# A fused attention and MLP kernel: key norms in the exp's scale, the first batch staged ahead of the weights, one copy per transposed tile, and another order around the layer norm

## The chip, the cores and the metric

The kernel runs on one core of a Trainium2 chip. Its time is the device time of one execution in microseconds. TensorE (PE) multiplies matrices and transposes, VectorE (DVE) works on tiles and reads PSUM, ScalarE (ACT) applies functions with a scale and a bias, GpSimd (POOL) works on SBUF and issues the weights' transfers, and SyncE (SP) issues most other transfers.

## The reference

Attention over 8 batches of 12 heads, 448 tokens and 64 dimensions, with q and k divided by their root mean square; then, over the 768 values of each token, a layer norm and an MLP with 3072 hidden values, added to its input.

```
q_n, k_n = rmsnorm(q, g_q), rmsnorm(k, g_k)     # x / sqrt(mean(x*x) + 1e-6) * g
scores = matmul(q_n, k_n.T) / 8;  attn = softmax(scores)
x = matmul(attn, v)                             # [8, 448, 768] after the heads are put side by side
xn = (x - mean) / sqrt(var + 1e-6) * g_ln
out = x + relu(xn @ w_ch1) @ w_ch2
```

## The kernel before

**Attention.** Two heads make a pair; there are 48 pairs, six for each batch. The 448 tokens of a head lie as 384 (three tokens on each of 128 partitions) and 64 left over, and the left-over tokens of two heads share a tile, so a pair has seven tiles of 128 keys. q, k and v come in *units*: one pair each in batch 0 (units 0 to 5), two pairs each later (`UNITS`). `load_unit` issues nine transfers for a unit, one large and two small ones for each of k, q and v. Batch 0's units use three places in the MLP buffer `hT` in turn, so unit 3 waits until unit 0 has been used up; later units have a pool of two (`p_in`).

`prep_ops` makes a unit ready: squares (ACT), sums (DVE), the product of k with both gains (`kg`, POOL), the reciprocal root (`root`: `_rsqrt`, an exp on the bits as a first guess, then six small VectorE steps), `kn` and `qn` (the scaled k and q), `khi` and `klo` (k split into two fp16 halves), `qdup` (q a second time, beside itself) and the copies of v (POOL). `trans_k` and `trans_q` transpose seven tiles on TensorE into one PSUM tile and copy them to SBUF with two and three copies. `scores(p, i)` multiplies one tile of 128 keys by 448 queries and takes the exp on ACT; `values(p, i)` multiplies the result by v, with a column of ones for the sum; after the seventh tile `evac_o` divides. `stats` takes the layer norm's statistics of that pair's 128 columns.

**MLP.** For batch b, `ln_ops` gives the statistics' root, then for each of 3 or 4 token tiles a normalisation (ACT, then DVE) and `ln_trans` (six transposes and a copy to `xnT`). An even batch has 3 token tiles; the left-over 64 tokens wait for the odd batch, which has 4. `mlp_chunks` is 24 *up* chunks (six matmuls, then a relu to `hT`) and 8 *down* chunks for each token tile (six matmuls each).

**Order.** PE, ACT, POOL and SP follow the order in which the program emits; VectorE's order is made by a scheduler. `attention` emits pairs in steps of one key tile: the scores of pair p beside the values of pair p-1, the next units' preparation at planned steps (`todo`). `run` emits attention through pair 6, then the layer norm of batch 0, and then for each batch its MLP chunks with attention steps between them, so that the next batch's attention is done when 0.82 of the chunks' cost (`frac`) is out; the layer norm of the next batch follows, spread over the rest. The weights are issued on POOL, w1 in three transfers and w2 in two, beside pairs 0 and 3.

Transfers from SP and ACT share eight semaphores (DMAHW0 to 7) in turn, so that each issue waits until the transfer eight places before it is complete.

Of the kernel before, what the change touches and what calls it, by code (L numbers as in the profile page):

```python
# [22 lines left out]
UNITS = [(0, 2 * i, 1) for i in range(NPAIR)]  # L23
# [5 lines left out]
REC_LO, REC_HI = 1.0 / 3.0e7, 0.5  # L29


def _rsqrt(nc, out, a, t, eps):

    eng = nc.vector
    eng.tensor_scalar(out=a, in0=a, scalar1=eps, scalar2=None, op0=ALU.add)
    nc.scalar.activation(out, a.bitcast(INT32), AFT.Exp, scale=-0.5 * LN2 * 2.0 ** -23,
                         bias=0.5 * LN2 * (127.0 - 0.043))
    for _ in range(2):
        eng.tensor_tensor(out=t, in0=out, in1=out, op=ALU.mult)  # L39
        eng.scalar_tensor_tensor(out=t, in0=t, scalar=-0.5, in1=a, op0=ALU.mult, op1=ALU.mult)  # L40
        eng.scalar_tensor_tensor(out=out, in0=t, scalar=1.5, in1=out, op0=ALU.add, op1=ALU.mult)
# [14 lines left out]
class _Fast:  # L56


    def __init__(self, ctx, tc, sh, q, k, v, g_ln, w1, w2, out):
# [21 lines left out]
        for t in self.kT:  # L81
            nc.vector.memset(t[:, 1], 0.0)
# [5 lines left out]
        nc.vector.memset(self.rec, 0.01)  # L88
        self.hT = fix.tile([128, NFF, 512], FP16, name="hT", tag="hT")
        self.xs, self.xls, self.st = {}, {}, {}  # L90
# [3 lines left out]
    def load_unit(self, u):  # L94
# [3 lines left out]
        if m == 1:  # L98
            o = 2688 * (u % 3)
            t = self.hT.rearrange("p f n -> p (f n)")[:, o:o + 2688].bitcast(FP32)  # L100
            t = t.rearrange("p (n g d) -> p n g d", n=3, d=D)
        else:
            t = self.p_in.tile([128, 3, 14, D], FP32, tag="qkv")
        eng = nc.scalar if u < 2 else nc.sync
        for n, src in ((1, self.k), (0, self.q), (2, self.v)):
            nc.sync.dma_start(
# [7 lines left out]
    def prep_ops(self, u):  # L114
# [8 lines left out]
        def begin():  # L123
# [3 lines left out]
            c["rt"] = self.p_n.tile([128, 2, 14], FP32, tag="rt", name="rt")[:, :, 0:g]  # L127
            c["qn"] = self.p_n.tile([128, 14, 2, D], FP16, tag="qn", name="qn")[:, 0:g]
# [12 lines left out]
        def root():  # L141
            _rsqrt(nc, c["rr"], c["ssq"], c["rt"], D * 1e-6)
# [6 lines left out]
        def kn():  # L149
            _scaled(nc, c["t"][:, 1], c["t"][:, 1], c["rr"][:, 1])  # L150

        def khi():
            nc.vector.tensor_copy(out=c["khl"][:, :, 0], in_=c["t"][:, 1])
# [5 lines left out]
        def qn():  # L159
            _scaled(nc, c["qn"][:, :, 0], c["t"][:, 0], c["rr"][:, 0])  # L160

        def qdup():
            nc.vector.tensor_copy(out=c["qn"][:, :, 1], in_=c["qn"][:, :, 0])
# [5 lines left out]
        def vleft():  # L169
            for e in range(2):  # L170
# [4 lines left out]
                lambda: (total(0), vmain()), root, None, kn, khi, klo, qn, qdup, vleft]  # L175


    def trans_k(self, p):
# [3 lines left out]
        ps = self.ps_tr.tile([128, 1024], FP16, tag="tr", name="psK")  # L182
        kT = self.kT[p % 2]
        gs = [6 * m + w] + [6 * w + i for i in range(6)]
        for i, g in enumerate(gs):
            nc.tensor.matmul(ps[:, ts(i, 128)], khl[:, g], sh.id16, is_transpose=True,  # L186
                             start=(i == 0), stop=(i == 6))
        flat = kT.rearrange("p g d -> p (g d)")
        nc.vector.tensor_copy(out=flat[:, 0:64], in_=ps[:, 0:64])
        nc.vector.tensor_copy(out=flat[:, 128:960], in_=ps[:, 64:896])  # L190

    def trans_q(self, p):
# [3 lines left out]
        ps = self.ps_tr.tile([128, 1024], FP16, tag="tr", name="psQ")  # L196
        qT = self.p_qT.tile([128, 896], FP16, tag="qT")
        gs = [6 * w, 6 * w + 1, 6 * w + 2, 6 * m + w, 6 * w + 3, 6 * w + 4, 6 * w + 5]
        for i, g in enumerate(gs):
            nc.tensor.matmul(ps[:, ts(i, 128)], qn[:, g], sh.id16,  # L200
                             is_transpose=True, start=(i == 0), stop=(i == 6))
        nc.vector.tensor_copy(out=qT[:, 0:448], in_=ps[:, 0:448])  # L202
        nc.vector.tensor_copy(out=qT[:, 448:832], in_=ps[:, 512:896])
        nc.vector.tensor_copy(out=qT[:, 832:896], in_=ps[:, 448:512])
        self.prs[p] = dict(qT=qT, kT=self.kT[p % 2])

    def scores(self, p, i):
# [11 lines left out]
        else:  # L219
            nc.tensor.matmul(ps[:, 0:S], kT[:, 0:128], qT[:, 0:S], start=True, stop=False)  # L220
            nc.tensor.matmul(ps[:, 0:S], kT[:, 64:192], qT[:, S:2 * S], start=False, stop=True)
        nc.scalar.activation(out=c["E"][:, i], in_=ps[:, 0:S], func=AFT.Exp, scale=1.0 / 8.0,  # L222
                             bias=EXP_BIAS)
# [44 lines left out]
    def attention(self):  # L268

        n, nu = B * NPAIR, len(UNITS)  # L270
        todo, last = {}, -9
        for u in range(1, nu):
            p, m = UNIT_PAIR[u], UNITS[u][2]
            st, e = max(7 * (p - 1 - m) + 2, last + 1), 7 * (p - 1) + 1
            last = e
            ops = self.prep_ops(u)
            for x, op in enumerate(ops):
                if op is not None:
                    todo.setdefault(max(0, st + (e - st) * x // (len(ops) - 1)), []).append(op)
            if u + 2 < nu and u + 2 > 2:  # L280
                todo.setdefault(max(0, e), []).append(lambda u=u: self.load_unit(u + 2))
        for u in range(3):
            self.load_unit(u)
        for op in self.prep_ops(0):
            if op is not None:
                op()
        self.trans_k(0)
        self.trans_q(0)
        for p in range(n + 1):
            b = p // NPAIR  # L290
            if p < n and p % NPAIR == 0:
                self.xs[b] = self.p_x.tile([128, 3, DM], FP32, tag="x", name="x")
                if b % 2 == 0:
                    self.xls[b // 2] = self.p_xl.tile([128, DM], FP32, tag="xl", name="xl")
            for i in range(7):
                for op in todo.pop(7 * p + i, ()):
                    op()
                if p < n:
                    self.scores(p, i)
                if p > 0:  # L300
                    for x in {0: (), 1: (0, 1)}.get(i, (i,)):
                        self.values(p - 1, x)
                if p > 1 and i == 1 and (p - 1) % NPAIR:
                    self.stats(p - 2)
                if p + 1 < n and i == 2:
                    self.trans_k(p + 1)
                if p + 1 < n and i == 4:
                    self.trans_q(p + 1)
                if p > 0 and p % NPAIR == 0 and i == 6:
                    self.stats(p - 1)  # L310
                yield p + (i + 1) / 7
# [7 lines left out]
    def load_w2(self, n0, n1):  # L319
        self.nc.gpsimd.dma_start(  # L320
            out=self.sh.w2[:, n0:n1],
            in_=self.w2[128 * n0:128 * n1].rearrange("(c p) d -> p c d", p=128))
# [8 lines left out]
    def stats(self, p):  # L331
# [3 lines left out]
        if hp == 0:  # L335
            self.st[b] = self.p_m.tile([128, 4, NPAIR * 6 + 2], FP32, tag="stat", name="stat",
                                       bufs=2)
        for t, x in enumerate(self.tok_tiles(b)):
            nc.vector.bn_stats(out=self.st[b][:, t, 6 * hp:6 * hp + 6],  # L339
                               in_=x[:, 128 * hp:128 * hp + 128])  # L340

    def ln_ops(self, b):
# [7 lines left out]
        mv = st[:, :, 6 * NPAIR:6 * NPAIR + 2]  # L350

        def root():
            c["rs"] = self.p_m.tile([128, 4], FP32, tag="rs", name="rs", bufs=2)
            c["sh"] = self.p_m.tile([128, 4], FP32, tag="sh", name="sh", bufs=2)
            for t in range(n):
                nc.vector.bn_aggr(out=mv[:, t], in_=st[:, t, 0:6 * NPAIR])
# [11 lines left out]
        res = [root, lambda: norm(0)]  # L368
        for t in range(1, n):
            res += [lambda t=t: norm(t), lambda t=t: self.ln_trans(c["xn", t - 1], t - 1)]  # L370
        return res + [lambda: self.ln_trans(c["xn", n - 1], n - 1)]
# [11 lines left out]
    def mlp_chunks(self, b):  # L383
# [32 lines left out]
        for t in range(n):  # L416
            for g in range(2):
                for s in range(4):
                    yield 6 * 160, (lambda t=t, g=g, s=s: down(t, g, s))
# [10 lines left out]
    def run(self):  # L430
        att = self.attention()
        self.pos = 0.0

        def upto(target):
            while self.pos < target:
                nxt = next(att, None)
                if nxt is None:
# [240 lines left out]
```

## Time and profile before

| | before |
|---|---|
| median of 3 runs (lowest to highest) | 733.85 us (733.62 to 735.27) |
| the profiled execution, its own time | 733.03 us |
| its span | 731.2 us |
| PE busy | 633.3 us (87%), 5066 matmuls |
| DVE busy | 428.0 us (59%) |
| ACT busy | 338.2 us (46%) |
| POOL busy | 89.7 us (12%) |
| mean granted clock of TensorE | 0.956 |
| DMA packets | 54.83 MB |

A page of the profile gives busy time per engine, the span in 40 slices of 18.3 us (each digit a busy share in tenths), the chain of waits that ended last, and groups of like instructions: line, engine, operation, tiles written and read, count, then busy time, mean of one in ns and the idle time before them with what ended it. In the waits, the name left of the arrow waited for the one right of it: total in us, times, longest. SPq, ACTq and PEq are the queues in which an engine issues transfers or waits.

### The profile page before, as it was taken

The numbers are of one execution on the slowest core, as the hardware profiler recorded it, in microseconds if no ns is written. First come the engines' busy times: TensorE is split into PE (matmuls) and PEld (weight loads), VectorE is DVE, ScalarE is ACT, GpSimd is POOL, SyncE is SP. The second block draws the span as 40 slices with busy tenths as digits, with TensorE's granted clock in tenths as the row PEclk, the third lists the DMA queues.
The fourth block names the chain that finished last, engine by engine and source line by source line (L and its number), as shares of the span: only waits on it lengthen the run. The fifth ranks groups of instructions, "written<-read, shape, count | busy, mean of one in ns | idle before, by whom it ended". The sixth has DMA issues, their size and how long they took to land.

```text
span 731.2 us, 12852 instructions
## 1 busy us (share of the span) xinstructions
PE 633.3 (87%) x5066; PEld 387.3 (53%) x5066; DVE 428.0 (59%) x1195; ACT 338.2 (46%) x646; POOL 89.7 (12%) x119
## 2 busy tenths in 40 slices
PE   0452458997999999997999999998999999979996
PEld 0231335664555666664556666654556566644463
DVE  1886688667466756776646757784565755351011
ACT  1443246753465327752665247633664356423400
POOL 1332012110101101110111011110111010000000
PEclk9997568998999999999999999998999999999999
DMA  4499951221322014230322123202313100000011
GB/s 138 95 220 219 229 150 48 53 77 44 98 77 74 26 44 106 70 99 22 98 76 78 44 85 110 77 23 70 99 28 98 44 22 2 23 23 22 1 44 46
DMA packets 69234, 54.83 MB, mean 75 GB/s; under 512 B 23216, under 2 KB 63152, under 8 KB 69168
## 3 DMA queue, kind: packets, MB, share of 16 engines
q1 hardware_dynamic: 62320, 43.86, 21.0%
q0 software_dynamic: 5456, 9.44, 7.0%
q8 instruction: 41, 0.67, 0.4%
q10 hardware_dynamic: 1392, 0.66, 0.3%
q14 instruction: 25, 0.20, 0.1%
HBM read 52.36 MB, written 11.01 MB: 87 GB/s over the span
## 4 chain that ended last, share of the span: by engine, by line
PE 74%; DVE 11%; DMA 6%; SPq 3%; ACT 3%; issue 1%; ACTq 0%; DVEq 0%
PE psH L394 30%; PE psC L405 25%; PE psS L217 6%; PE oA L241 4%; SPq L111 3%; PE psQ L200 2%; DMA t<-in_k_dram 2%; PE psK L186 2%; DMA hT<-in_q_dram 2%; PE psX L379 2%; PE oB L243 1%; DMA hT<-in_v_dram 1%; ACT t L364 1%; DVE xn L366 1%; DVE x L258 1%
## 5 line engine op out<-in xcount | busy, mean ns | idle before, releaser
L405 PE MATMUL psC<-w,hT 128*128 128x384 f16 x1344 | 246.8, 332 | 0.0
L394 PE MATMUL psH<-xnT,w 128*128 128x512 f16 (+1 forms) x1152 | 245.2, 352 | 1.2 <-DVE xnT L381 1.2
L222 ACT ACTIVATE E<-psS 128x448 f16<-128x448 f32 x336 | 179.1, 540 | 119.9 <-PE psS L217 99.1
L396 ACT ACTIVATE hT<-psH 128x384 f16<-128x384 f32 (+1 forms) x192 | 104.5, 544 | 149.7 <-PE psH L394 148.2
L405 PEld LDWEIGHTS <-hT 128*128 128x128 f16 x1344 | 127.7, 100 | 75.8 <-issue 6.2
L394 PEld LDWEIGHTS <-w 128*128 128x128 f16 x1152 | 105.0, 98 | 81.7 <-issue 1.3
L217 PE MATMUL psS<-qT,kT 128*128 128x448 f16 x288 | 105.3, 373 | 8.0 <-ACT E L222 5.2
L241 PEld LDWEIGHTS <-E 128*128 128x128 f16 x1008 | 74.4, 101 | 68.5 <-issue 20.8
L145 POOL TENSOR_TENSOR t<-t,gprod 128x896 f32<-128x896 f32 x21 | 43.7, 2081 | 455.0 <-issue 271.7
L241 PE MATMUL oA<-v,E 128*128 128x65 f16 x864 | 70.7, 198 | 9.9 <-DVE x L258 9.5
L409 DVE TENSOR_TENSOR x<-psC,x 128x384 f32<-128x384 f32 x48 | 26.7, 556 | 83.3 <-PE psC L405 82.9
L186 PE MATMUL psK<-id,khl 128*128 128x128 f16 x336 | 29.2, 232 | 43.6 <-DVE rt L39 23.6
L243 PE MATMUL oB<-v,E 128*128 128x65 f16 x288 | 53.5, 197 | 0.3
L186 PEld LDWEIGHTS <-khl 128*128 128x128 f16 x336 | 21.5, 104 | 44.9 <-issue 23.8
L139 DVE TENSOR_REDUCE ssq<-khl 128x14 f32<-128x896 f32 (+1 forms) x27 | 26.4, 979 | 26.3 <-ACT khl L136 25.8
L202 DVE COPY qT<-psQ 128x448 f16<-128x448 f16 x48 | 18.7, 389 | 38.6 <-PE psQ L200 38.6
L217 PEld LDWEIGHTS <-kT 128*128 128x128 f16 x288 | 29.2, 103 | 22.5 <-DVE qT L202 2.3
L256 DVE RECIPROCAL rec_all<-oA 128x6 f32<-128x6 f32 x48 | 9.3, 193 | 49.3 <-PE oA L241 49.2
L379 PE MATMUL psX<-id,xn 128*128 128x128 f16 x168 | 15.7, 243 | 22.6 <-DVE xn L366 22.6
L339 DVE BATCH_NORM_STATS2 stat<-x 128x6 f32<-128x128 f32 x144 | 34.5, 282 | 0.7
L243 PEld LDWEIGHTS <-E 128*128 128x128 f16 x336 | 33.3, 99 | 1.4 <-DVE xl L263 0.9
L200 PE MATMUL psQ<-id,qn 128*128 128x128 f16 x336 | 29.2, 232 | 4.9 <-DVE kT L190 4.9
(75 smaller groups left out, 594.8 us busy)
## 6 DMA issues: line engine op xcount, KB each, us to landing
out_dram<-x SPq DMA_DIRECT2D x24, 384.0 KB, 2.3
t<-in_k_dram SPq DMA_DIRECT2D x21, 384.0 KB, 3.6
t<-in_q_dram SPq DMA_DIRECT2D x21, 384.0 KB, 4.1
t<-in_v_dram SPq DMA_DIRECT2D x21, 384.0 KB, 4.4
w<-in_moe_w_ch_dram POOLq DMA_DIRECT2D x3, 1536.0 KB, 21.0
w<-in_moe_w_ch_dram POOLq DMA_DIRECT2D x2, 2304.0 KB, 38.1
out_dram<-xl SPq DMA_DIRECT2D x8, 192.0 KB, 3.0
t<-in_k_dram SPq DMA_DIRECT2D x42, 32.0 KB, 3.4
```

The lines of the kernel that those rows point to most:

```text
L145: nc.gpsimd.tensor_tensor(out=c["t"][:, 1], in0=c["t"][:, 1], in1=sh.gprod.unsqueeze(1).broadcast_to([128, g, D]), op=ALU.mult)
L186: nc.tensor.matmul(ps[:, ts(i, 128)], khl[:, g], sh.id16, is_transpose=True, start=(i == 0), stop=(i == 6))
L200: nc.tensor.matmul(ps[:, ts(i, 128)], qn[:, g], sh.id16, is_transpose=True, start=(i == 0), stop=(i == 6))
L217: nc.tensor.matmul(ps[:, 0:S], kT[:, 192 + 128 * i:320 + 128 * i], qT[:, h * S:(h + 1) * S], start=True, stop=True)
L222: nc.scalar.activation(out=c["E"][:, i], in_=ps[:, 0:S], func=AFT.Exp, scale=1.0 / 8.0, bias=EXP_BIAS)
L241: nc.tensor.matmul(oA[:, t, cs], E[:, i, ts(t, 128)], rhs, start=(i == 0 and t == 0), stop=(i == 6 and t == 2))
L243: nc.tensor.matmul(oB[:, cs], E[:, i, 320:448], rhs, start=(i == 0), stop=(i == 6))
L339: nc.vector.bn_stats(out=self.st[b][:, t, 6 * hp:6 * hp + 6], in_=x[:, 128 * hp:128 * hp + 128])
L379: nc.tensor.matmul(ps[:, dc], xn[:, ts(dc, 128)], sh.id16, is_transpose=True, start=(dc == 0), stop=(dc == NDC - 1))
L394: nc.tensor.matmul(ps[:, 0:N], sh.w1[:, dc, ts(f, 128)], xnT[:, dc, 0:N], start=(dc == 0), stop=(dc == NDC - 1))
L396: nc.scalar.activation(out=hT[:, f, 0:N], in_=ps[:, 0:N], func=AFT.Relu)
L405: nc.tensor.matmul(ps[:, 0:384], hT[:, f, ts(t, 128)], sh.w2[:, f, ts(g, 384)], start=(f == 0), stop=(f == NFF - 1))
```

## The change

It has these parts:

- **Key norms.** k is no longer scaled (`kn` goes). The reciprocal root goes to a tile that is kept (`rr_all`, from `_rsqrt`'s new `last`), and the exp of `scores` takes its column for these 128 keys as scale, where it had the constant 1/8. `khi` moves from DVE to ACT and, with `klo`, no longer needs the root. `qdup` goes to POOL for units 0 to 3.
- **Staging.** Batch 0 has four units (one, one, two and two pairs). Units 0 to 2 get places of their own in `hT`, unit 3 and unit 4 go to `p_in`, and all five are issued at the start. ACT issues only unit 0's q; a first exp (`warm`) brings the table load forward; the layer norm's gain is issued behind unit 3. w1 follows at step 2 and w2 at step 21; w2 is loaded by halves of its columns, and batch 0's down chunks take all token tiles of the first half first.
- **Copies.** One PSUM tile (`tr`) is kept for both transposes. The left-over tile is written in two parts, to where it belongs, and one copy takes the whole: 960 columns for k, 896 for q (on ACT for pairs 0, 2 and 4).
- **Order.** Only the six pairs of batch 0 come before its layer norm. `frac` is 0.77. The layer norm's root and first two normalisations come as soon as attention is done; the transposes come last, one ahead of each of the last chunks. Statistics are taken of 256 columns, after every second pair.
- **Flag.** The check of the sums, by which the general path is chosen at the end, also checks the kept roots against `gmax`, and stands after the third chunk of the last MLP.

The core of the diff:

```diff
-UNITS = [(0, 2 * i, 1) for i in range(NPAIR)]
+UNITS = [(0, 0, 1), (0, 2, 1), (0, 4, 2), (0, 8, 2)]
...
-        if m == 1:
-            o = 2688 * (u % 3)
-            t = self.hT.rearrange("p f n -> p (f n)")[:, o:o + 2688].bitcast(FP32)
+        if u < 3:
+            o = 2688 * u
+            t = self.hT.rearrange("p f n -> p (f n)")[:, o:o + 2688 * m].bitcast(FP32)
...
-        eng = nc.scalar if u < 2 else nc.sync
         for n, src in ((1, self.k), (0, self.q), (2, self.v)):
-            nc.sync.dma_start(
+            eng = nc.scalar if u == 0 and n == 0 else nc.sync
+            eng.dma_start(
...
-        def kn():
-            _scaled(nc, c["t"][:, 1], c["t"][:, 1], c["rr"][:, 1])
-
         def khi():
-            nc.vector.tensor_copy(out=c["khl"][:, :, 0], in_=c["t"][:, 1])
+            nc.scalar.activation(c["khl"][:, :, 0], c["t"][:, 1], AFT.Identity)
...
-                lambda: (total(0), vmain()), root, None, kn, khi, klo, qn, qdup, vleft]
+                lambda: (total(0), vmain()), khi, root, klo, None, qn, qdup, vleft]
...
-        nc.vector.tensor_copy(out=flat[:, 0:64], in_=ps[:, 0:64])
-        nc.vector.tensor_copy(out=flat[:, 128:960], in_=ps[:, 64:896])
+        nc.vector.tensor_copy(out=kT.rearrange("p g d -> p (g d)"), in_=ps[:, 0:960])
...
+        if p in (0, 2, 4):
+            nc.scalar.copy(out=qT, in_=ps.rearrange("p e s -> p (e s)"))
+        else:
+            nc.vector.tensor_copy(out=qT, in_=ps.rearrange("p e s -> p (e s)"))
...
-        nc.scalar.activation(out=c["E"][:, i], in_=ps[:, 0:S], func=AFT.Exp, scale=1.0 / 8.0,
-                             bias=EXP_BIAS)
+        nc.scalar.activation(out=c["E"][:, i], in_=ps[:, 0:S], func=AFT.Exp,
+                             scale=self.rr[:, 1, g:g + 1], bias=EXP_BIAS)
...
+        todo.setdefault(2, []).append(lambda: [self.load_w1(c, c + 1024) for c in range(0, FF, 1024)])
+        todo.setdefault(21, []).append(lambda: [self.load_w2(g) for g in range(2)])
...
+            for u in range(3):
+                self.load_unit(u)
+            for op in self.prep_ops(0):
+                if op is not None:
+                    op()
+            self.trans_k(0)
+            self.trans_q(0)
+            self.load_unit(3)
+            self.nc.sync.dma_start(self.sh.gln, self.g_ln.unsqueeze(0).broadcast_to([128, DM]))
+            self.load_unit(4)
...
-        frac = 0.82
+        frac = 0.77
...
+                if items and len(chunks) - i <= len(items):
+                    items.pop(0)()
                 emit()
                 done += cost
...
+                if self.pos >= goal and items is None:
+                    items = self.ln_ops(b + 1)
+                    items.pop(0)()
```

Where instructions stand, at three places. First, ScalarE from its start: `gg` and `gln` are the gains, `hT` holds the loaded unit, `khl` and `qn` take the squares, `rr` the root's first guess, `E` the exp. Before:

```order
L632 DMA gg_65<-in_g_q_dram 128x64
L633 DMA gg_65<-in_g_k_dram 128x64
L442 DMA gln_70<-in_moe_g_ln_dram 128x768
L111 DMA hT_124<-in_k_dram 64x64 x2
L111 DMA hT_124<-in_q_dram 64x64 x2
L111 DMA hT_124<-in_v_dram 64x64 x2
...
L136 ACT_TABLE_LOAD
L136 ACTIVATE khl_157<-hT_124 128x448
L136 ACTIVATE qn_156<-hT_124 128x448
L36 ACTIVATE rr_154<-ssq_153 128x2x7
```

Of the change:

```order
L668 DMA gg_66<-in_g_q_dram 128x64
L669 DMA gg_66<-in_g_k_dram 128x64
L677 ACT_TABLE_LOAD
L677 ACTIVATE warm_65<-ones_63 128x1
L109 DMA hT_128<-in_q_dram 128x2x192
L114 DMA hT_128<-in_q_dram 64x64 x2
L141 ACTIVATE khl_162<-hT_128 128x448
L141 ACTIVATE qn_161<-hT_128 128x448
L155 ACTIVATE khl_162<-hT_128 128x7x64
L37 ACTIVATE rr_159<-ssq_158 128x2x7
L205 COPY qT_191<-tr_129 128x896
```

Fifteen transfers stood ahead of the first square (the dots leave out six small loads of unit 1); now five do, and the table load stands ahead of three of them.

Second, SyncE at unit 3's loads, with the semaphores that each waits for. Before:

```order
L106 DMA hT_124<-in_k_dram 128x2x192 [waits DMAHW6_49,DVE_49]
L111 DMA hT_124<-in_k_dram 64x64 [waits DMAHW7_49]
L111 DMA hT_124<-in_k_dram 64x64 [waits DMAHW0_49]
L106 DMA hT_124<-in_q_dram 128x2x192 [waits DMAHW1_49,Activation_49]
L111 DMA hT_124<-in_q_dram 64x64 [waits DMAHW2_49]
L111 DMA hT_124<-in_q_dram 64x64 [waits DMAHW3_49]
L106 DMA hT_124<-in_v_dram 128x2x192 [waits DMAHW4_49,Pool_49]
```

Of the change:

```order
L109 DMA t_200<-in_k_dram 128x4x192 [waits DMAHW5_49]
L114 DMA t_200<-in_k_dram 64x2x64 [waits DMAHW6_49]
L114 DMA t_200<-in_k_dram 64x2x64 [waits DMAHW7_49]
L109 DMA t_200<-in_q_dram 128x4x192 [waits DMAHW0_49]
L114 DMA t_200<-in_q_dram 64x2x64 [waits DMAHW1_49]
L114 DMA t_200<-in_q_dram 64x2x64 [waits DMAHW2_49]
L109 DMA t_200<-in_v_dram 128x4x192 [waits DMAHW3_49]
```

The waits for VectorE, ScalarE and GpSimd, which had to be done with unit 0, are gone; those for earlier transfers stay.

Third, TensorE at the end of MLP(0): `oB` are the last values of batch 1's attention, `psC` the MLP's down matmuls, `psX` the layer norm's transposes. Before:

```order
L243 MATMUL oB_1812<-vl_115,E_1628 128x130
L405 LDWEIGHTS hT_124
L405 MATMUL psC_1890<-w2_73,hT_124 128x384
...
L405 MATMUL psC_1961<-w2_73,hT_124 128x384
...
L379 LDWEIGHTS xn_1958
L379 MATMUL psX_1979<-id16_58,xn_1958 128x128
```

Of the change:

```order
L248 MATMUL oB_1665<-vl_120,E_1506 128x130
L447 LDWEIGHTS hT_128
L447 MATMUL psC_1726<-w2_78,hT_128 128x384
...
L447 MATMUL psC_1801<-w2_78,hT_128 128x384
...
L421 LDWEIGHTS xn_1774
L421 MATMUL psX_1829<-id16_58,xn_1774 128x128
...
L447 MATMUL psC_1841<-w2_78,hT_128 128x384
...
L421 MATMUL psX_1848<-id16_58,xn_1778 128x128
```

Between `oB` and the first `psX` there were 18 matmuls on `psC`, and there are 42 now; behind that twelve stood between two token tiles' transposes, and now six.

244 lines of the change are left out of this document (132 added, 112 removed).

## The prediction

> **What bounds the kernel now.** I read the busy slices of the page first, then cut the span into stages.
>
> ```profile
> PE   0452458997999999997999999998999999979996
> ```
>
> TensorE is short of work in the first six slices and full almost everywhere after them. The windows by stage (columns: length, busy time of PE, PEld, DVE, ACT and POOL, granted clock, DMA share, GB/s) say the same in numbers; the cuts are the first exp, the first MLP matmul, and the starts of MLP(1), MLP(2) and MLP(3).
>
> ```profile
> 0.00:28.40 28.40, 2.38 (x16) 1.70 (x17) 12.89 (x42) 3.69 (x7) 4.68 (x14) 1.00 0.38 107
> 28.40:117.55 89.15, 44.63 (x390) 28.89 (x389) 66.75 (x187) 39.93 (x79) 24.30 (x33) 0.77 0.90 186
> 117.55:189.77 72.22, 67.56 (x563) 43.34 (x563) 48.23 (x138) 36.55 (x72) 6.74 (x8) 0.95 0.17 50
> 189.77:273.95 84.18, 83.33 (x657) 48.90 (x655) 51.27 (x139) 42.79 (x79) 10.12 (x12) 1.00 0.23 69
> 273.95:347.77 73.82, 69.38 (x613) 45.27 (x612) 51.94 (x146) 40.90 (x80) 10.11 (x12) 0.98 0.26 73
> ```
>
> Up to 117.55 us PE has only 47.0 us of work, at a mean clock of 0.77 in the second stage; behind that it is busy for 83.33 of 84.18 us. So only two things can be won: the start, and the few waits later. TensorE's waits up to 117.55 (first two rows) and after it (third row) name them.
>
> ```profile
> PE psK L186 <- DVE rt L39: 23.6, 1, 23.6
> PE psK L186 <- DVE khl L156: 20.0, 3, 13.8
> PE psX L379 <- DVE xn L366: 19.7, 7, 4.4
> ```
>
> What stands behind the 20.0 us is shown by the chain of waits from 0 to 120 us (start, length, what):
>
> ```profile
> 14.46 1.28 ACT L136
> ...
> 32.31 9.12 DMA hT<-in_v_dram
> 41.44 11.79 DMA hT<-in_q_dram
> 53.25 4.49 SPq L111
> ...
> 59.86 6.53 SPq L111
> ...
> 73.76 16.33 DMA t<-in_k_dram
> ```
>
> From 32 to 90 us the path is loads of q, k and v and SyncE's queue, not arithmetic. The timeline shows who slows them: the weights start at 31.06, and the nine transfers of one two-pair unit then take from 67.71 to 89.39 (21.7 us) to be issued, against 103.01 to 109.87 (6.9 us) when the weights have landed.
>
> ```profile
> 31.06 2.66 POOL L315 DMA_DIRECT2D w<-in_moe_w_ch_dram  x3
> 67.71 1.19 SPq L106 DMA_DIRECT2D t<-in_k_dram  x1
> 89.39 0.46 SPq L106 DMA_DIRECT2D t<-in_k_dram  x1
> 103.01 0.37 SPq L106 DMA_DIRECT2D t<-in_k_dram  x1
> 108.63 1.24 SPq L111 DMA_DIRECT2D t<-in_v_dram  x2
> ```
>
> **Part 1, the first exp.** The order rows show twelve small loads ahead of ScalarE's first computation (14.46 in the chain); now there are three loads of q, with the table load ahead of them. Rows for the steps that remain:
>
> ```profile
> 28.40 0.98 ACT L222 ACTIVATE E<-psS 128x448 f16<-128x448 f32 x2 [7.39 <-PE psS L217]
> hT<-in_q_dram ACTq DMA_DIRECT2D x4, 16.0 KB, 2.4
> L136 ACT ACTIVATE khl<-hT 128x448 f32<-128x448 f32 x6 | 3.4, 571 | 0.0
> L139 DVE TENSOR_REDUCE ssq<-qn 128x7 f32<-128x448 f32 x6 | 3.6, 606 | 0.0
> L39 DVE TENSOR_TENSOR rt<-rr 128x14 f32<-128x14 f32 x12 | 2.6, 215 | 1.1 <-ACT rr L36 0.9
> 23.59 0.91 PE L186 MATMUL psK<-id,khl 128*128 128x128 f16 x7 [23.59 <-DVE rt L39]
> ```
>
> q's last piece is issued near 6 us, behind two loads, the 1.28 us table load and two lane waits, and lands 2.4 later, at 8.4. Then: square 0.57, total 0.61, add and exp of the root 0.5, six root steps 1.3, qn 0.6, its copy on GpSimd 0.6, seven transposes 0.91, the one copy on ScalarE about 1.0: 6.1, so 14.5. On ScalarE unit 1's two squares, its khi (behind 1.1 us of GpSimd) and its root stand ahead of the first exp: another 3. I take **17.5 us** instead of 28.40; ends 14.5 (unit 1 wholly hidden) and 21 (its loads late by 3.5).
>
> **Part 2, six pairs.** Batch 0 now has all its loads issued ahead of the weights, which wait on GpSimd behind unit 2's gprod product (some 22 us). Units 0 to 2 need 24 issues of about 0.6 us; unit 3's nine come next, about 17 to 23 us, mostly before the weights, and ScalarE wants it after nine exps (about 26 us). So the 20.0 us and the long chain pieces should go. What paces the pairs then is ScalarE:
>
> ```profile
> L222 ACT ACTIVATE E<-psS 128x448 f16<-128x448 f32 x336 | 179.1, 540 | 119.9 <-PE psS L217 99.1 <-PE psS L221 20.5
> L136 ACT ACTIVATE khl<-t 128x896 f32<-128x896 f32 x21 | 19.8, 945 | 10.5 <-DMA t<-in_k_dram 10.5
> L364 ACT ACTIVATE t<-x,sh,rs 128x768 f32<-128x768 f32 x24 | 23.9, 1022 | 11.7 <-DVE sh L358 11.0
> ```
>
> The exp gets its scale from a tile, which no row of before shows for exp. The nearest row is L364, with scale and bias from tiles: 1022 ns for 768 columns, where squares of 448 and 896 columns (571, 945) give 838 by interpolation, 184 more for two tile operands. One operand costs between 0 and 184; I take the middle, 92. The Trainium skill (ScalarE: Activation LUTs, What ACT_TABLE_LOAD costs) states about 93 ns for each such operand; by that rule 336 exps cost ScalarE 31 us more, which speaks against the change, and by a price of 0 nothing; the trace's middle agrees with the rule.
>
> Batch 0 on ScalarE: 42 exps of 0.60 (two pipelined ones take 0.98 now, so 0.5 and 0.09), four squares and two khi of 0.95, two qT copies of 0.9, two roots of 0.2: 33 us, 5.5 a pair. VectorE had 66.75 us for eight pairs, 8.3 a pair, and loses kn, khi, three of five PSUM copies, half the statistics' instructions and here qdup. So the pace lies between 5.5 and 8.3; I take 6.5, since neither engine waits for loads any more but TensorE starts at half clock (0.91 us for seven transposes). Last exp: 17.5 + 39 = **56.5**.
>
> qdup of four units goes to GpSimd. A row shows what that can do to VectorE:
>
> ```profile
> 36.25 1.17 POOL L145 TENSOR_TENSOR hT<-hT,gprod 128x448 f32<-128x448 f32 x1 [1.55 <-issue]
> 36.38 1.52 DVE L156 TENSOR_TENSOR khl<-hT,khl 128x448 f16<-128x448 f32 x1
> L156 DVE TENSOR_TENSOR khl<-hT,khl x6: 608/622/1519, 22.8 to 77.1; 128x448 f16<-128x448 f32 x6
> ```
>
> Beside a GpSimd product the same subtraction takes 1.52 instead of 0.62. Four copies can cost up to 4 x 0.9 = 3.6 us, or nothing; this is inside the pace. The Trainium skill (SBUF — State Buffer, Who interferes with whom) says that a VectorE instruction with two SBUF inputs and a GpSimd one that reads SBUF block each other for the whole instruction; by it the sum is up to 3.6 us worse, without it unchanged. The row agrees.
>
> **Part 3, to MLP(0).** Before, the last pair's reciprocal to the first MLP matmul took 117.55 - 103.75 = 13.8 us, with exps between:
>
> ```profile
> 103.75 0.18 DVE L256 RECIPROCAL rec_all<-oA 128x6 f32<-128x6 f32 x1
> ```
>
> Now no exp stands between, but unit 4's squares do. I take 13.5 (10 to 15): MLP(0) starts at **70** (62 to 82, from the ends above, which won't all fall together).
>
> MLP(0) in turn gets more attention: 42 exps precede it, not 56, so 7 pairs fall into it instead of 5. The price of a pair on TensorE: MLP(7), without attention, is 62.4 us by the chain,
>
> ```profile
> 662.29 31.19 PE psH L394 x144
> 693.47 31.21 PE psC L405 x192
> ```
>
> and MLP(1), the same size with six pairs, 84.18: less 0.7 of waits and 1 of LN transposes, 20.1, so 3.35 a pair. MLP(0) has three quarters of the size: 46.8 + 7 x 3.35 + 1.4 transposes + 1.5 at a slow clock + 1.2 LN wait = **74.4** (the same sum for before gives 71.3 against 72.22). MLP(1) starts at 144.4 instead of 189.77: **45.4 us won**.
>
> **Part 4, the LN stretches.** After an even batch, TensorE runs out of chunks, waits 4.44 us for xn, and then runs slow:
>
> ```profile
> 172.40 3.09 PE L405 MATMUL psC<-w,hT 128*128 128x384 f16 x18
> 179.93 0.82 PE L379 MATMUL psX<-id,xn 128*128 128x128 f16 x6 [4.44 <-DVE xn L366]
> 180.54 4.05 PE L405 MATMUL psC<-w,hT 128*128 128x384 f16 x12
> ...
> 187.66 2.11 PE L405 MATMUL psC<-w,hT 128*128 128x384 f16 x12
> ```
>
> Twelve matmuls take 4.05 instead of 2.11. By the order 42 MLP matmuls (6.8 us), not 18, now stand between the last values and the first transposes; needed are 7.5 us and about 0.5 for the wider statistics. Some 1.2 of wait stays and the clock should hold. Later than 189.77 that is three times 4.44 + 1.6, three waits of 0.66 after odd batches and 1.5 around MLP(7): 21.6, less 3.6 that stays: **18 us won**. If the cover failed, all of it stays. LN instructions of later tiles hide behind one chunk each.
>
> **Part 5, what gets dearer.** ScalarE gains 31 us of exps and 21 khi (20 us). In a stage like 273.95 its 40.90 busy us become about 40.90 + 3.9 + 2.9 = 48 of 70, but attention is packed into 0.77 of the chunks and the relus into the first half, so in bursts TensorE may wait for an exp: I add **2 us** in all (0 to 15). VectorE only loses work. The weights' second half now comes in shorter rows; first used some 35 us after MLP(0) starts, it is hidden.
>
> **Sum:** 731.2 - 45.4 - 18 + 2 = 669.8 of span; the profiled execution took 733.03, 1.83 more: 671.6, say **672**. The median, 733.85, is 0.1% above the profiled run, which I leave out.
>
> **Rivals.** (a) *Loads stay late*: the change staged batch 0 ahead, but units 3 and 4 are still in flight when the weights start, and at 21.7 us a unit ScalarE, in order, stands before unit 3's square. For: the 73.76 piece is just that. Against: unit 3 is issued by 23 us. It decides if the weights go out before 18 us; price 15 us: 687. Chance 0.12. (b) *ScalarE paces the MLP stages*: for, bursts of square, khi and dearer exps between relus; against, 48 of 70 us. At 3 us for each of seven stages 693 less the 2 booked: 691. Chance 0.08. (c) *LN waits remain* because xn comes later than 42 matmuls cover: 690. Chance 0.05. (d) *Slower than before*: the tile scale makes each exp so long that ScalarE bounds every stage. Two stages hold 84 exps and some 44 us of other ScalarE work and would last 146 us; to lose the 62 us won, they must last 164, so 1.42 us an exp. L364, with two such operands, needs 1.02 for 768 columns. Chance 0.02; time from 734. (e) *Better*: pairs at 5.5 and no bursts, 660 or less: 0.05.
>
> **Chances.** Forecast 0.68; (a) to (e) 0.32. A difference under 0.2% can't be told from none. Faster 0.97, same 0.01, slower 0.02. The range 656 to 692 takes in the ends of the start (8 us early with a fast pace, 12 late), (a), (b) and (c).
>
> **What would show it.** Right: first exp near 17.5, first MLP matmul near 70, no load on the chain after 30 us, MLP(1) near 144, psX waits under 6 us in sum, psC after them at 2.1 for twelve. Exps at about 0.63. Wrong: a DMA piece over 5 us in the chain between 20 and 60 us, ScalarE among TensorE's releasers inside the MLP stages, or psX waits still over 3 us each.

## The result and the profile after

| kernel | median us | range | runs | ratio to before |
|---|---|---|---|---|
| before | 734.21 | 733.62 to 735.27 | 4 | 1 |
| changed | 672.12 | 671.77 to 672.22 | 4 | 0.9152 (95%: 0.9136 to 0.9168) |
| changed, run again with the experiments | 672.31 | 672.27 to 673.05 | 4 | 0.9146 (0.9132 to 0.9160) |

The forecast was 672.0 us. The profiled execution of the changed kernel has a span of 670.2 us. In the page's busy slices TensorE has 1, 6, 8, 3 and 8 tenths of work in the first five, where the first six had 0, 4, 5, 2, 4 and 5, and is full from there to the tail:

```profile
PE   1683899999999999999999999999999999999995
```

The windows by stage, cut as before at the first exp, the first MLP matmul and the starts of MLP(1), MLP(2) and MLP(3), with one more cut at the end of the last exp of batch 0 (columns: length, busy time of PE, PEld, DVE, ACT and POOL, granted clock, DMA share, GB/s):

```profile
0.00:16.84 16.84, 2.76 (x16) 1.69 (x17) 7.88 (x25) 5.77 (x11) 4.83 (x13) 1.00 0.56 148
16.84:52.00 35.16, 25.26 (x256) 15.76 (x255) 26.03 (x63) 30.56 (x53) 15.15 (x18) 1.00 1.04 219
52.00:67.09 15.09, 4.50 (x46) 3.42 (x47) 11.54 (x31) 5.93 (x8) 4.10 (x4) 0.52 1.22 220
67.09:144.60 77.51, 74.23 (x649) 47.67 (x649) 57.77 (x134) 52.38 (x94) 13.57 (x16) 0.98 0.58 126
144.60:227.80 83.20, 83.07 (x656) 49.08 (x654) 45.59 (x106) 48.51 (x82) 10.12 (x12) 1.00 0.23 70
227.80:297.64 69.84, 68.36 (x614) 44.49 (x612) 46.78 (x110) 46.26 (x83) 10.11 (x12) 1.00 0.27 77
```

MLP(1) starts at 144.60, where it started at 189.77: of the 61.0 us of span that were won (731.2 - 670.2), 45.2 lie ahead of it and 15.8 behind it (541.4 against 525.6). Inside batch 0 ScalarE is busy for 30.56 of 35.16 us, more than any other engine (the run with a constant scale below shows that it doesn't set the pace alone); transfers run at 219 GB/s beside it without standing in the way. The chain of waits shows only two pieces of DMA up to 70 us, and both are early loads; before, load after load stood there up to 90.

```profile
2.52 3.57 DMA hT<-in_v_dram
...
11.81 1.22 DMA hT<-in_k_dram
...
16.24 0.59 ACT khl L155
...
49.02 1.71 ACT E L227 x3
```

In TensorE's list of waits the LN transposes (psX) have fallen from 22.6 us in 9 waits to 10.7 in 6, of which 8.7 are the two of LN(0).

```profile
PE psX L421 <- DVE xn L401: 10.7, 6, 6.6
```

The timeline of TensorE shows the rest: in front of MLP(1) 42 matmuls of the down product now cover all but 0.50 us of the wait, and the six behind it take 1.14, so the clock holds. The last two rows are LN(0)'s longer wait and the first MLP matmul:

```profile
131.61 6.99 PE L447 MATMUL psC<-w,hT 128*128 128x384 f16 x42
139.10 0.51 PE L421 MATMUL psX<-id,xn 128*128 128x128 f16 x6 [0.50 <-DVE xn L401]
139.44 1.14 PE L447 MATMUL psC<-w,hT 128*128 128x384 f16 x6
61.29 1.74 PE L421 MATMUL psX<-id,xn 128*128 128x128 f16 x12 [6.62 <-DVE xn L401]
67.09 4.39 PE L436 MATMUL psH<-xnT,w 128*128 128x384 f16 x18 [1.18 <-DVE xnT L423]
```

The price of the norm in the exp's scale stands in the group of the exps, 633 ns where it was 540:

```profile
L227 ACT ACTIVATE E<-psS,rr_all 128x448 f16<-128x448 f32 x336 | 208.4, 633 | 67.8 <-PE psS L220 51.4
```

### The profile page after: what moved, and what is told of

It reads as the page before. It is cut to its first block, busy times and chain, and to the rows that moved or that the text cites. A ratio compares the mean times of both kernels' runs of the same rounds, so it can differ in the third digit from the quotient of the medians.

```text
span 670.2 us, 12546 instructions
## 1 busy us (share of the span) xinstructions
PE 620.5 (93%) x5066; PEld 379.5 (57%) x5066; DVE 373.8 (56%) x886; ACT 384.3 (57%) x669; POOL 91.6 (14%) x115
## 4 chain that ended last, share of the span: by engine, by line
PE 79%; DVE 10%; ACT 5%; issue 2%; SPq 1%; DMA 1%; POOL 0%; DVEq 0%
PE psH L436 30%; PE psC L447 27%; PE psS L220 7%; PE oA L246 4%; PE tr L202 2%; PE tr L189 2%; ACT E L227 2%; ACT khl L155 2%; PE oB L248 2%; DVE xn L401 1%; PE psS L223 1%; PE psS L224 1%; PE psX L421 1%; DVE stat L374 1%; ACT t L399 1%
## 5 line engine op out<-in xcount | busy, mean ns | idle before, releaser
L227 ACT ACTIVATE E<-psS,rr_all 128x448 f16<-128x448 f32 x336 | 208.4, 633 | 67.8 <-PE psS L220 51.4
L447 PE MATMUL psC<-w,hT 128*128 128x384 f16 x1344 | 239.3, 326 | 0.0
L447 PEld LDWEIGHTS <-hT 128*128 128x128 f16 x1344 | 125.4, 98 | 72.4
L220 PE MATMUL psS<-qT,kT 128*128 128x448 f16 x288 | 101.7, 360 | 9.8 <-ACT E L227 7.5
L191 DVE COPY kT<-tr 128x960 f16<-128x960 f16 x48 | 31.5, 655 | 40.1 <-PE tr L189 39.6
L207 DVE COPY qT<-tr 128x896 f16<-128x896 f16 x45 | 28.0, 622 | 29.9 <-PE tr L202 29.6
L158 DVE TENSOR_TENSOR khl<-t,khl 128x896 f16<-128x896 f32 x22 | 24.0, 1091 | 18.0 <-ACT khl L155 17.8
L144 DVE TENSOR_REDUCE ssq<-qn 128x14 f32<-128x896 f32 (+1 forms) x25 | 26.2, 1046 | 10.1 <-ACT qn L141 9.1
L401 DVE TENSOR_TENSOR xn<-t,gln 128x768 f16<-128x768 f32 x28 | 26.9, 968 | 8.8 <-ACT t L399 8.8
L399 ACT ACTIVATE t<-x,sh,rs 128x768 f32<-128x768 f32 x24 | 23.8, 1021 | 13.0 <-DVE sh L393 12.3
```

Of the source, the lines that this page charges most:

```text
L144: nc.vector.tensor_reduce(out=c["ssq"][:, n], in_=c["sq", n], axis=AX.X, op=ALU.add)
L191: nc.vector.tensor_copy(out=kT.rearrange("p g d -> p (g d)"), in_=ps[:, 0:960])
L220: nc.tensor.matmul(ps[:, 0:S], kT[:, 192 + 128 * i:320 + 128 * i], qT[:, h * S:(h + 1) * S], start=True, stop=True)
L399: nc.scalar.activation(out=t32, in_=tiles[t], func=AFT.Identity, scale=c["rs"][:, t:t + 1], bias=c["sh"][:, t:t + 1])
L401: nc.vector.tensor_tensor(out=c["xn", t], in0=t32, in1=sh.gln, op=ALU.mult)
L447: nc.tensor.matmul(ps[:, 0:384], hT[:, f, ts(t, 128)], sh.w2[:, f, ts(g, 384)], start=(f == 0), stop=(f == NFF - 1))
```

## The experiments

Ratios are to the kernel before, run on the same chip; 0.001 is 0.73 us. "The changed kernel" stands at 0.9152 or 0.9146 (above).

**1. The LN order alone, in both directions.** First in the kernel before: the transposes last in the tail, the attention packed into 0.77 of the chunks; batch 0 keeps the old order.

```diff
-        res = [root, lambda: norm(0)]
...
+        return [first] + [lambda t=t: trans(t) for t in range(n)]
...
-        frac = 0.82
+        frac = 0.77
```

> The kernel before with part 4 alone: layer-norm root and first two normalisations as soon as attention is done, transposes last, frac 0.77. Theory (the parts add, and the layer-norm stretches are worth 4 transitions of 4.4 + 1.6 us and 3 of 0.66, less 0.5 that stays at each of four): about 24 us less than before, 710 us (706 to 715). Rival (denser attention at 0.77 gives back what the shorter waits win, since ScalarE or VectorE then pace it): 720 or more.

Measured: 708.15 us, ratio 0.9618 (0.9595 to 0.9641), 27.8 us won, inside the expected range. In the list of waits those for xn fall from 22.6 us to 4.1:

```profile
PE psX L391 <- DVE xn L366: 4.1, 5, 1.6
```

Then the same taken out of the changed kernel:

> The changed kernel with part 4 undone: old spreading of the layer norm behind attention, frac 0.82. Theory: the waits of 4.4 us (now 5 with the wider statistics) and the slow clock behind them come back at four places, so 672 + 22 = 694 us (690 to 698). Rival (VectorE, with 54 us less to do, brings xn early enough by itself): below 682.

Measured: 700.18 us, ratio 0.9512 (0.9494 to 0.9531): some 27 us lost, more than the 22 that was expected and past the range of 690 to 698. The list of waits has the total, the timeline one of the waits after odd batches:

```profile
PE psX L426 <- DVE xn L401: 32.5, 9, 6.7
```

```profile
228.83 0.57 PE L426 MATMUL psX<-id,xn 128*128 128x128 f16 x6 [2.26 <-DVE xn L401]
```

After odd batches the old order waits 2.26 us in the changed kernel, 0.66 in the kernel before: three times 1.6, or 4.8 us of the 27. What a step brought and what its return costs are two numbers. Less that, 22 us stand in one direction and 28 in the other.

**2. The key norms.** Norms back on VectorE, with the f16 copy of k (khi) back on VectorE too, and the constant in the exp:

```diff
+        def kn():
+            _scaled(nc, c["t"][:, 1], c["t"][:, 1], c["rf"][:, 1])
...
-            nc.scalar.activation(c["khl"][:, :, 0], c["t"][:, 1], AFT.Identity)
+            nc.vector.tensor_copy(out=c["khl"][:, :, 0], in_=c["t"][:, 1])
...
-                lambda: (total(0), vmain()), khi, root, klo, None, qn, qdup, vleft]
+                lambda: (total(0), vmain()), root, kn, khi, klo, None, qn, qdup, vleft]
...
-                             scale=self.rr[:, 1, g:g + 1], bias=EXP_BIAS)
+                             scale=1.0 / 8.0, bias=EXP_BIAS)
```

> The changed kernel with the key norms undone: kn again on VectorE, khi on VectorE behind it, constant scale 1/8 in the exp. Theory: nothing changes in the MLP stages, where TensorE is full; in batch 0 VectorE gets 1.7 us more for each two pairs and the first exp waits some 1.5 us longer, while ScalarE is freed of 42 x 0.09 and two khi: 674 to 678 us. Rival (the dearer exp and khi on ScalarE cost TensorE waits in every stage): faster than 671.

Measured: 687.68 us, ratio 0.9342 (0.9324 to 0.9359), 14 us lost: a miss. The first exp comes at 20.09, the last one of batch 0 ends at 62.2, so a pair takes 7.0 us instead of 5.86. In the profiled runs 11.2 us are lost by the start of MLP(1) (155.88, against 144.71 in the changed kernel run again) and 4.5 behind it, where the theory expected nothing. The timeline of VectorE at unit 1's norms shows no idle time, and a subtraction beside a GpSimd product of 2.07 us that takes 2.37:

```profile
21.52 0.63 DVE L49 SCALAR_TENSOR_TENSOR hT<-hT,rr_all 128x448 f32<-128x448 f32 x1
22.07 0.62 DVE L49 SCALAR_TENSOR_TENSOR qn<-hT,rr_all 128x448 f16<-128x448 f32 x1
22.60 0.61 DVE L158 CAST khl<-hT 128x448 f16<-128x448 f32 x1
23.13 1.08 DVE L144 TENSOR_REDUCE ssq<-khl 128x14 f32<-128x896 f32 x1
24.12 2.37 DVE L161 TENSOR_TENSOR khl<-hT,khl 128x448 f16<-128x448 f32 x1
```

So VectorE is full at this place, with 1.2 us of norms and copy more for each unit of one pair; over the six pairs it is busy for 31.6 of 42.1 us, the most of any engine. The next run leaves the norms in the exp and gives back khi alone (of that diff only the line with `AFT.Identity` and the one that replaces it):

> The changed kernel with one step given back: the copy of k to f16 (khi) on VectorE as before the change, 0.6 us there, and no longer 0.95 us on ScalarE; the key norms stay in the exp's scale. It parts the two things that the run without key norms undid together (14 us slower). Theory (what costs there is the product with the norms, which waits for the root and stands ahead of klo and the transposes, so that the whole chain of a unit gets longer): khi alone changes little, ratio 0.911 to 0.919, first exp within 1 us. Rival (VectorE's added time is what costs, whichever operation brings it): half of the 14 us or more, ratio 0.922 or more.

Measured: 682.57 us, ratio 0.9273 (0.9260 to 0.9285), 9 us lost, so the theory fell and the rival's number came. The group of these copies tells what they do on VectorE at this place, and the list of waits who then waits:

```profile
L155 DVE CAST khl<-t 128x896 f16<-128x896 f32 x22 | 26.2, 1189 | 19.0 <-POOL t L150 12.0 <-DMA t<-in_q_dram 3.7 <-DMA t<-in_v_dram 2.3
```

```profile
PE oA L246 <- DVE x L263: 10.4, 10, 2.5
```

The copy waits 12.0 us in all for GpSimd's product, and VectorE's queue with it; then it takes 1189 ns beside GpSimd's copies of v, which come next there, where the same copy took 617 in the kernel before. The one of the 22 copies that has no GpSimd work beside it, at 70.98, took 609. TensorE waits 10.4 us for VectorE's outputs of attention (1.5 in the changed kernel). All of the loss has come by MLP(1), which starts at 155.30; how it splits between the waiting and the longer copy is not shown. This run puts khi ahead of the root, where the change has it; before, it stood behind kn, so the run doesn't price the engine at the old place, and its 9 us are no share of the 14.

The price of the longer exp by itself, with the constant scale in the changed kernel; this run leaves the key norms out of the scores:

> The changed kernel with the exp's scale as a constant 1/8 (the key norms are left out of the scores, so the result is not the reference's). Theory: exp goes from 633 back to 540 ns; in batch 0, where ScalarE is busy 30.6 of 35.2 us, 42 x 0.09 = 3.9 us are saved nearly whole, in the MLP stages at most 1: 668 to 669.5 us. Rival (ScalarE's price is hidden everywhere): 671.5 to 672.5. Rival (ScalarE paces the MLP stages): 660 or less.

Measured: 670.95 us, ratio 0.9120 (0.9102 to 0.9139): about 2 us by the ratios, with intervals that overlap the changed kernel's slightly, and short of the 668 to 669.5 us expected. Exps have a median of 543 ns against 634. Of 31 us on ScalarE, about 2 are seen; MLP(1) starts 0.8 earlier (143.84), the rest comes later. Between the first and the last exp of batch 0 ScalarE's busy time falls from 30.56 to 27.38 us, but the stretch only from 35.16 to 34.79: ScalarE is the busiest engine there, and yet doesn't set the pace alone.

**3. The loads.** All weights ahead of the first batch's loads, which makes rival (a) happen:

```diff
-        todo.setdefault(2, []).append(lambda: [self.load_w1(c, c + 1024) for c in range(0, FF, 1024)])
-        todo.setdefault(21, []).append(lambda: [self.load_w2(g) for g in range(2)])
...
         def first():
+            for c in range(0, FF, 1024):
+                self.load_w1(c, c + 1024)
+            for g in range(2):
+                self.load_w2(g)
             for u in range(3):
                 self.load_unit(u)
```

> The changed kernel with all weights issued ahead of the first batch's loads. Theory (the weights' late issue is what takes the loads off the path; this is rival (a) made to happen on purpose): units 1 to 3 are issued at some 20 us a unit beside the weights, so the first exp comes at 25 us or later, a DMA piece of over 5 us stands in the chain between 15 and 60 us, and MLP(0) starts 10 to 25 us later than 67: 682 to 700 us. Rival (the gain of the start comes from the fewer and earlier operations ahead of the exps, and the transfers were hidden by then): first exp within 2 us of 16.84, MLP(0) within 3 us of 67, 671 to 676 us.

It is compared with the changed kernel, run again beside it:

> The changed kernel once more, beside the other kernels of this call, so that they are compared with it on one chip. Expected 0.915 of the kernel before (0.9136 to 0.9168 so far), that is 670 to 675 us with a kernel before of 733 to 737.

672.31 us for the changed kernel, 702.12 for this one, ratio 0.9550 (0.9535 to 0.9565): 30 us lost, just past the far end of the theory. The first exp is at 28.50, MLP(0) starts at 96.99 instead of 67.13, so that all of the loss lies ahead of it, and the chain has its loads back:

```profile
3.29 12.66 DMA hT<-in_v_dram
...
16.91 9.98 DMA hT<-in_q_dram
...
33.33 13.82 DMA hT<-in_v_dram
47.17 11.23 DMA t<-in_q_dram
```

So the place of the weights' issue is worth up to 30 us (before, they went out behind units 0 to 2, so its own place was less extreme) of the 45 that the start won. The staging in the MLP buffer lets the loads go out early; that alone would not do if the weights went out ahead of them.

**4. Copies and qdup.** Five copies of PSUM a pair again, all on VectorE:

```diff
-        nc.vector.tensor_copy(out=kT.rearrange("p g d -> p (g d)"), in_=ps[:, 0:960])
+        nc.vector.tensor_copy(out=flat[:, 0:128], in_=ps[:, 0:128])
+        nc.vector.tensor_copy(out=flat[:, 128:960], in_=ps[:, 128:960])
...
+        for a, z in ((0, 448), (448, 832), (832, 896)):
+            nc.vector.tensor_copy(out=qT[:, a:z], in_=src[:, a:z])
```

> The changed kernel with five copies of PSUM to SBUF per pair instead of two (two for k, three for q), all of them on VectorE. Theory (VectorE's copies matter only in the first batch, where two engines share the pace): three more fixed costs a pair and the three qT copies back from ScalarE, some 1 us a pair of VectorE, of which half shows: 1 to 4 us slower than the changed kernel, by the time between the first and the last exp; nothing from the MLP stages. Rival (transposes wait for their PSUM tile, which is only one now, all along): TensorE's waits for the copies grow by over 0.3 us in each of 24 pairs, 8 us or more.

Measured: 674.73 us, ratio 0.9173 (0.9160 to 0.9185), about 2 us lost. The theory's size holds, its place only in part: MLP(0) starts 0.8 us later (67.90), MLP(1) 2.2 later (146.87), and nothing more is lost behind it. And qdup of units 0 to 3 on VectorE:

```diff
-            (nc.gpsimd if u < 4 else nc.vector).tensor_copy(out=c["qn"][:, :, 1],
+            nc.vector.tensor_copy(out=c["qn"][:, :, 1],
```

> The changed kernel with qdup of units 0 to 3 on VectorE, not GpSimd (0.56 and 0.93 us there). Theory (a GpSimd operation beside a VectorE one costs up to 0.9 us each, four times; the forecast set 0 to 3.6 us for it, inside the pace): what VectorE is given, four copies of some 0.3 to 0.4, is about what the collisions took: within 1.5 us of the changed kernel, ratio 0.913 to 0.917. Rival (GpSimd's hop delays the transposes of q and so the first exp): 2 us or more faster, first exp 0.4 us or more earlier, ratio under 0.912.

Measured: 675.40 us, ratio 0.9177 (0.9165 to 0.9190), about 2 us lost, just past the theory's bound; the rival did not come. The theory has the collisions on the wrong side. Two of the four copies stand beside GpSimd's product for the next unit and take 1.60 and 1.70 us on VectorE, while the other two take 0.28 and 0.38:

```profile
20.76 1.60 DVE L165 COPY qn<-qn 128x448 f16<-128x448 f16 x1
29.64 1.70 DVE L165 COPY qn<-qn 128x896 f16<-128x896 f16 x1
```

TensorE waits 4.9 us for these copies, where it waited 1.6 us for GpSimd's. In the changed kernel no VectorE instruction beside GpSimd's qdup is visibly longer than others of its kind, so the move took the collisions away.

**5. What is still to be had.** Between the last exp of batch 0 and the first MLP matmul the changed kernel prepares unit 4, ahead of LN(0)'s copies. Here that preparation is spread over the last two pairs of batch 0:

```diff
+            st, e = max(7 * (p - 1 - m) + 2, last + 1, 0), 7 * (p - 1) + 1
             if p == nb0:
-                continue
-            st, e = max(7 * (p - 1 - m) + 2, last + 1, 0), 7 * (p - 1) + 1
+                st, e = 28, 7 * nb0 - 1
...
-                steps += [[op] for op in self.prep_ops(UNIT_PAIR.index(nb0)) if op is not None]
-                steps[-1].append(lambda: self.load_unit(6))
```

> The changed kernel with unit 4 (the first of batch 1) prepared inside batch 0 (its steps spread over the last two pairs of that batch) and not behind it. Theory (its squares and sums on VectorE and ScalarE stand ahead of LN(0)'s copies and lengthen the stretch from the last exp to the first MLP matmul, 15.1 us where 13.5 was forecast, and then delay the first pair inside MLP(0)): the stretch falls to 12 to 13.5 us, the first exp to the last grows by up to 2 us, 2 to 5 us faster than the changed kernel. Rival (batch 0 is paced by the same two engines, so what leaves the stretch comes back between the exps): within 1 us of the changed kernel.

Measured: 674.65 us, ratio 0.9175 (0.9161 to 0.9189): no gain, and about 2 us lost, which neither the theory nor its rival had. The stretch from the last exp of batch 0 to the first MLP matmul does not shrink to 12 or 13.5 us; it grows to 18.0 (59.23 to 77.20). The edit also does more than its name says: five exps of batch 1 now come ahead of MLP(0), between LN(0)'s steps, where none did. The row of ScalarE in the timeline names what delays it: the square of q waits for a load that is still in flight beside the weights.

```profile
49.30 0.95 ACT L141 ACTIVATE qn<-t 128x896 f32<-128x896 f32 x1 [3.27 <-DMA t<-in_q_dram]
```

In the changed kernel unit 4's issues run late too, from 22.76 to 41.40; the place of its preparation hides that. So the next run moves the first weights (w1) as well:

```diff
-        todo.setdefault(2, []).append(lambda: [self.load_w1(c, c + 1024) for c in range(0, FF, 1024)])
+        todo.setdefault(9, []).append(lambda: [self.load_w1(c, c + 1024) for c in range(0, FF, 1024)])
```

> The changed kernel with unit 4 prepared inside batch 0, as in the run that came out no faster (its chain holds 5.80 us of SyncE's queue and a 9.79 us piece of unit 4's k, in flight beside the weights), and with the first weights' issue moved from step 2 to step 9, behind unit 4's loads. Theory (only that late load ate the gain): no DMA piece over 3 us in the chain between 30 and 66 us, MLP(1) starts at 138 to 143 where it started at 144.7, ratio to the kernel before 0.903 to 0.911 where the changed kernel has 0.9146. Rival (batch 0 is paced by VectorE and ScalarE, so work moved into it comes back): ratio 0.913 to 0.918, MLP(1) at 144 to 147. A third way (the weights come too late): TensorE waits for w in MLP(0), slower than 0.918.

Measured: **669.40 us, ratio 0.9093 (0.9081 to 0.9106)**, faster than both kernels, some 4 us under the changed one by the ratios and 2.9 by the medians. Unit 4 is now issued from 23.89 to 31.31, the wait for q is gone, and MLP(1) starts at 142.63 (144.71 in the changed kernel run again). The last DMA piece of over 3 us in its chain ends at 29.75, as the theory has it; before it the chain is SyncE's queue, issue behind issue:

```profile
23.26 0.59 SPq L304
24.37 5.38 DMA t<-in_k_dram
29.77 0.94 ACT qn L141
```

The gain is not the shorter stretch that was looked for: from the last exp of batch 0 to the first MLP matmul it is still 18.6 us (54.99 to 73.58). But with attention of batch 1 in between, TensorE waits 3.6 us for LN(0)'s xn instead of 8.7, and MLP(0), with less attention left, lasts 69.05 us instead of 77.58. The later weights without the early unit 4 were not run.

Last, unit 1's first operations ahead of the first transposes, and v loaded one unit later:

```diff
-            for u in range(3):
-                self.load_unit(u)
+            self.load_unit(0, (1, 0))
+            for u in (1, 2):
+                self.load_unit(u, (1, 0))
+                self.load_unit(u - 1, (2,))
+            self.load_unit(2, (2,))
...
+            for op in early:
+                op()
```

> The fastest version so far (unit 4 inside batch 0, weights behind its loads) with two more edits of the start: the v of units 0 to 2 is loaded one unit later, so that k and q of unit 1 land earlier, and unit 1's two squares, its gprod product and its k total are issued ahead of the first transposes, where ScalarE waited some 3.9 us for them. Theory (the first exp waits for unit 1's operations that stand ahead of it on ScalarE, not for its own inputs): first exp 1 to 2.5 us earlier than 17.6, MLP(1) at 139.5 to 141.7 where it started at 142.6, ratio 0.905 to 0.909. Rival (v then comes late for GpSimd, which holds it in order ahead of qdup, or the squares hold up unit 0's root): no gain or a loss, ratio 0.910 or more.

Measured: 670.48 us, ratio 0.9122 (0.9109 to 0.9136), no faster than the run before it (1.1 us slower by the medians, about 2 by the ratios); the rival holds. The first exp came only 0.8 us earlier (16.80). VectorE, in order, took unit 1's sums between the root steps of unit 0, and GpSimd waited for v:

```profile
10.31 0.17 DVE L40 TENSOR_TENSOR rt<-rr 128x14 f32<-128x14 f32 x1
10.52 0.62 DVE L147 TENSOR_REDUCE ssq<-khl 128x7 f32<-128x448 f32 x1
11.05 0.17 DVE L41 SCALAR_TENSOR_TENSOR rt<-rt,ssq 128x14 f32<-128x14 f32 x1
11.13 0.61 DVE L147 TENSOR_REDUCE ssq<-qn 128x7 f32<-128x448 f32 x1
10.30 0.55 POOL L172 CAST v<-hT 128x384 f16<-128x384 f32 x1 [2.01 <-DMA hT<-in_v_dram]
```

The operations did leave ScalarE's way, but unit 0's own chain got longer by 1.0 us: ScalarE's copy of its qT starts at 15.27, where it started at 14.31.

## Why the prediction was right, point by point

- **The bound** was read rightly: early loads and LN waits held nearly all that could be won. Putting the weights first costs 30 us, undoing the LN order 27.
- **Part 1, the first exp:** 17.5 forecast, 16.84 measured (17.5 in the second run). The squares of unit 1 ahead of it were named, and the last experiment shows they are not the whole of it.
- **Part 2, the pace:** 6.5 us a pair forecast, 35.16 / 6 = 5.86 measured, near the lower bound of 5.5 that was ScalarE's. The reason is only in part that bound: with 3.2 us less on ScalarE the six pairs were only 0.4 us shorter. The exp's tile scale was forecast at 92 ns and measured at 633 - 540 = 93. The Trainium skill (ScalarE: Activation LUTs, What ACT_TABLE_LOAD costs) gives about 93 ns for such an operand; the trace agrees. The up to 3.6 us for qdup's collisions did not appear; they come when qdup is on VectorE, as the run with it there shows.
- **What Part 2 mis-valued** is the move of kn and khi. It was put down as busy time that VectorE loses. The runs show 14 us for both, net of the dearer exp that comes with the change, and 9 for khi alone, at its new place: it counted what VectorE does, not what waits in its queue behind an operation that waits for GpSimd, nor that the copy itself gets longer beside GpSimd's. The number came out because the pace was set from bounds that a VectorE freed of both can reach.
- **Part 3, MLP(0):** forecast to start at 70 and to last 74.4; it started at 67.09 and lasted 77.51, so MLP(1) came at 144.60 against 144.4. That is so close by luck: two errors cancel, the six pairs 3.8 us faster than forecast and what follows them slower. The LN stretch was 15.09, not 13.5: unit 4's sums stand between LN(0)'s copies on VectorE at 62.15 and 65.03, 1.00 us each. And MLP(0) holds 3.3 us in which TensorE is idle (77.51 - 74.23), where the sum had 1.2, for LN alone; by the list of waits in that window, it waits for exps (1.5), for kT (1.3) and for xn (0.5). The other 1.0 is TensorE's own work. The chain in LN(0):

```profile
62.15 1.00 DVE ssq L144
63.18 0.56 DVE xnT L423
63.73 1.29 DVE xn L401
65.03 1.00 DVE ssq L144
```

- **Parts 4 and 5:** 18 won less 2 for ScalarE gives 16 behind MLP(1); measured 15.8. This is in part luck as well: the LN order alone, in the kernel before, took some 20 us off the span behind MLP(1) (541.4 to 521.3), so the rest of the change costs some 4 there, not 2, and what makes up those 4 is not shown. The cover of 42 matmuls holds (0.50 us of wait after an even batch, none after an odd one) and the clock stays up. The dearer exps cost about 2 us by the run with a constant scale, as booked, though half of it ahead of MLP(1).
- **Rivals:** none came. Rival (a) is real when the weights go first, and its price is 30 us, not 15, which reckoned with one unit late where all of batch 0's are.
- **Signs:** most came as named, two did not. TensorE's waits for xn sum to 10.7 us, not under 6, because LN(0)'s grew from 2.8 to 8.7. And ScalarE, a sign of being wrong, does stand among TensorE's releasers inside the MLP stages, though for only 2.2 us in 7 waits.

## What to carry over

Value a step that leaves an in-order engine by what waits behind it and what runs beside it, not by its busy time alone: a 0.6 us copy that waits for another engine's product, and then runs beside that engine's next copies, cost 9 us, all of it ahead of MLP(1). When loads compete with a large transfer for the same path, the issue order of the large one is the first thing to set, and any work moved forward must be checked against when its own load lands. An edit that fails by itself can help with another: unit 4 early lost about 2 us and, with the weights late, won 3 to 4 (the late weights by themselves were not run).

## What the runs showed of the hardware that was not expected

- The copy of 896 columns from f32 to f16 on VectorE took 617 ns in the kernel before and 1189 ns where it stands behind GpSimd's product with GpSimd's copies beside it, one after the other (1216 ns in the median). The Trainium skill (SBUF — State Buffer, Who interferes with whom) counts copies and casts in VectorE's two-port modes among the instructions that block each other with GpSimd's; the trace agrees in the time. The subtraction of 448 columns took 2.37 us beside a product of 2.07 us, where 0.62 is its time alone; the forecast had 1.52 as the longest such row. The copy of q of 448 columns, f16 to f16, took 1.60 us beside a product of 2.29 us and 0.28 without one.
- The old LN order, which waits 0.66 us after odd batches in the kernel before, waits 2.26 in the changed one with the same tiles; which operations stand ahead of xn there was not tried.
